# A mixed attention and long-convolution kernel on one core: another order, other slots and other engines for the same 1808 steps

## The chip, the core and the metric

The kernel runs on one core of a Trainium2 chip. The metric is the device time of one execution in microseconds; the median over several executions is compared. The core has a matrix engine (PE, with its weight loads shown apart as PEld), a vector engine (DVE), a scalar engine (ACT), a general engine (POOL), and a sync engine (SP) whose queue issues the transfers here.

## The reference, cut to what matters

Two branches read the same input x (2048 tokens, 512 channels) and a gate per token mixes them.

```
def reference(A_x, A_wq, ..., gate_w):
    def _A_ref(x, wq, wk, wv, wo, beta):       # attention with a memory, 32 heads, 4 segments of 512
        ...
        for s in range(N):
            logits = einsum('bhqd,bhkd->bhqk', qs, ks) * scale + mask
            p = softmax(logits)
            a_dot = einsum('bhqk,bhkd->bhqd', p, vs)
            a_mem = (phi(qs) @ M) / (phi(qs) @ z + 1e-6)
            outs.append(g * a_mem + (1.0 - g) * a_dot)
            M, z = M + phi(ks)^T vs, z + sum(phi(ks))
        return stack(outs) @ wo
    def _B_ref(u, A_re, ..., Dskip):           # a convolution over all 2048 tokens, per channel
        K = einsum('dn,dnl,dn->dl', Cc, exp(dt * A * l), dB).real
        y = irfft(rfft(u padded) * rfft(K padded))[:L]
        return y + u * Dskip
    g = sigmoid((x * gate_w).sum(-1))
    return g * _A_ref(x, ...) + (1 - g) * _B_ref(x, ...)
```

## The kernel before

`build_graph` writes the whole computation down as 1808 steps. A step belongs to an engine and is one instruction on ACT, DVE, POOL or SP, or a short run of matmuls on PE. 611 steps are on PE, 537 on DVE, 142 on ACT, 257 are transfers issued by SP, 6 are on POOL, and 255 are evictions or copies that may run on ACT or on DVE.

A step names the tiles that it reads and writes. A tile lies in a pool with a fixed number of slots (for PSUM, one or two of the eight banks, or four banks for the scores). Nothing decides at run time: the text `ORDER` lists the steps with the slots that each takes for the first time, and for the movable ones the engine, `a` for ACT and `v` for DVE. So `267a` is step 267 on ACT, and `1244/5/0` is step 1244, which takes slot 5 of its first new tile and slot 0 of its second. `replay` walks this list, gives out the slots, and appends each step to its engine's program. `emit` then turns every dependency, on data and on the last users of a slot, into waits on semaphores. Each engine runs its own program in the order of the list; between engines only the semaphores order anything.

The names (tags) of the steps that the text below speaks of:

- `prm`, `dt`, `prep`: the convolution's parameters, their exponentials and sines. `pow0.k` and `pow1.k`: repeated squares (ACT squares, L850; DVE the rest, L851 and L852). `pwc`: their copies to bf16 (L858, L859), with a transfer that swaps halves. `cb`: the products of B and C.
- `xl1.b`: the first step of the transform of x; evictions by `evac` (L229 on ACT, L230 on DVE), then a transfer to a scratch tensor in memory. Two slots take turns. `xTl1` to `xTl3`: x transposed by transfer (L743).
- `tabc0` to `tabc3`, `tab`, `lag`: tables of powers, built by DVE (L1346, L1349, L1355, L1358), and products of them.
- `tok`, `pk`, `pq`, `st`, `gate`: projections, memory state and gate of a segment. `sc`: scores on PE into four banks, exponential on ACT (L1190 and L1237). `mk`: mask on DVE (L1249). `pv`, `nrm`: product with the values and division (L1151 to L1154). `mem`, `oT`: memory read and transposed output.
- `X`, `E`, `K`, `Y`, `V` with 0 to 31: the convolution. X and K are made on PE and evicted, Y is their product on DVE (L1487), V the way back on PE, evicted and moved by a transfer into the tile V2.
- `fin`, `fir`, `fih`, `fis`, `xD`, `spl`, `out` with 0 to 15: the output tiles. `fin` and `fih` are the output projection, `fir` and `fis` the last step of the convolution. Eight of them are split, with a partial sum by DVE (L1521 for xD, L1543 for spl, L1557 for out); the other eight are scaled on their way out by ACT (L232) or DVE (L233).

PE's steps share line L706, the helper that issues a matmul.

## Time and profile before

| | us |
|---|---|
| median of 3 runs | 287.87 |
| lowest and highest | 287.21, 294.32 |
| span of the profiled execution | 287.5 |
| DVE busy in it | 265.0 |
| ACT busy in it | 254.6 |
| PE busy in it | 253.1 |

The profiled execution's span, from its first to its last instruction, is 287.5 us, 0.4 us under the median of the runs. Busy times are sums over one engine's instructions, without overlap. An idle time in the tables stands with what ended it: `7.3 <-PE psum L706 6.0` means 7.3 us of idle time ahead of these instructions, 6.0 of them ended by a matmul.

### The profile page before, as it was taken

The page shows a single profiled execution, that of the slowest core. Times are in us where ns is not written, and L with a number is a line of the kernel's source. Part 1 is how long each engine was busy: PE and PEld are TensorE (multiplying, and loading weights), DVE is VectorE, ACT ScalarE, POOL GpSimd, SP SyncE. Part 2 cuts the span into 40 slices and gives each one's busy share as a digit, 9 for nine tenths or more (in the row PEclk, how much of TensorE's full clock was granted, in tenths as well). Part 3 has the DMA queues.
Part 4 walks back from the last instruction along what each step waited for, and adds up shares of the span by engine and source line. Part 5 has one row for each costly group of instructions (what it writes and reads, how often), then busy time and mean ns, then how long its engine had stood idle before and what let it go on. Part 6 is the DMA issues. An engine that isn't in the chain of part 4 may idle for free.

```text
span 287.5 us, 9336 instructions
## 1 busy us (share of the span) xinstructions
PE 253.1 (88%) x3896; PEld 158.7 (55%) x3947; DVE 265.0 (92%) x617; ACT 254.6 (89%) x320; POOL 5.0 (2%) x10
## 2 busy tenths in 40 slices
PE   5767888787898989979999989999999999999992
PEld 2424454564556546756766657665555454555661
DVE  3998999999999999979999999999999999997782
ACT  5998999999999999989989999999999999983212
POOL 5000000000000000000000000000000000000000
PEclk9999899999999999979999999999999999999999
DMA  6996762421125256914643388585776795894224
GB/s 164 270 223 143 184 203 84 130 87 42 41 47 134 63 141 205 226 32 97 188 132 102 90 252 244 166 232 161 234 215 168 207 229 160 243 186 102 72 109 182
DMA packets 60187, 44.49 MB, mean 155 GB/s; under 512 B 36209, under 2 KB 53490, under 8 KB 60146
## 3 DMA queue, kind: packets, MB, share of 16 engines
q1 hardware_dynamic: 60146, 43.90, 57.0%
q8 instruction: 31, 0.51, 0.8%
q14 instruction: 10, 0.08, 0.1%
HBM read 22.09 MB, written 7.86 MB: 104 GB/s over the span
## 4 chain that ended last, share of the span: by engine, by line
ACT 35%; PE 28%; DVE 26%; issue 5%; DMA 3%; SPq 0%; DVEq 0%; ACTq 0%
PE psum L706 28%; ACT sb L1237 10%; ACT sb L229 10%; ACT sb L1190 8%; DVE sb L1346 7%; DVE sb L1355 3%; ACT sb L850 3%; DVE sb L230 2%; DMA sb<-sb 2%; DVE sb L1349 2%; DVE sb L1487 2%; DVE sb L1358 2%; DVE sb L1249 1%; DVE sb L1154 1%; ACT sb L1021 1%
## 5 line engine op out<-in xcount | busy, mean ns | idle before, releaser
L706 PE MATMUL psum<-sb 128*128 128x17 bf16 (+17 forms) x3808 | 247.4, 229 | 23.5 <-ACT sb L1190 7.4
L706 PEld LDWEIGHTS psum<-sb 128*128 128x128 bf16 (+6 forms) x3859 | 153.5, 102 | 115.5 <-issue 20.7
L229 ACT ACTIVATE sb<-psum 128x512 bf16<-128x512 f32 (+4 forms) x155 | 87.7, 624 | 7.6 <-PE psum L706 6.4
L1237 ACT ACTIVATE sb<-psum 128x2048 bf16<-128x2048 f32 x40 | 76.0, 1899 | 2.1 <-PE psum L706 1.7
L1190 ACT ACTIVATE sb<-psum 128x2048 bf16<-128x2048 f32 (+1 forms) x40 | 70.1, 1751 | 2.8 <-PE psum L706 2.7
L1346 DVE TENSOR_TENSOR sb<-sb 128x4096 bf16<-128x4096 bf16 (+3 forms) x24 | 37.7, 1569 | 0.0
L230 DVE CAST sb<-psum 128x512 bf16<-128x512 f32 (+1 forms) x49 | 29.9, 626 | 1.1 <-PE psum L706 0.9
L1355 DVE TENSOR_TENSOR sb<-sb 128x512 bf16<-128x512 bf16 (+1 forms) x48 | 25.0, 537 | 0.1
L1249 DVE TENSOR_TENSOR sb<-sb 128x1024 bf16<-128x1024 bf16 (+1 forms) x40 | 22.6, 577 | 0.2
L1487 DVE TENSOR_TENSOR sb<-sb 128x1024 bf16<-128x1024 bf16 x32 | 21.6, 685 | 0.9 <-ACT sb L229 0.5
L1349 DVE TENSOR_TENSOR sb<-sb 128x2048 bf16<-128x2048 bf16 (+3 forms) x24 | 20.7, 861 | 0.0
L232 ACT ACTIVATE sb<-psum,sb 128x512 bf16<-128x512 f32 x6 | 4.0, 687 | 12.3 <-PE psum L706 12.3
L1154 DVE TENSOR_TENSOR sb<-psum,sb 128x256 bf16<-128x256 f32 x32 | 13.3, 417 | 0.3
L1358 DVE TENSOR_TENSOR sb<-sb 128x512 bf16<-128x512 bf16 (+1 forms) x24 | 12.9, 536 | 0.0
L850 ACT ACTIVATE sb<-sb 128x512 f32<-128x512 f32 x18 | 11.8, 660 | 0.0
L1151 DVE RECIPROCAL sb<-psum 128x16 f32<-128x16 f32 x32 | 7.9, 252 | 1.8 <-PE psum L706 1.7
L1291 DVE TENSOR_TENSOR sb<-psum,sb 128x512 bf16<-128x512 f32 x12 | 8.2, 687 | 0.2
L858 ACT ACTIVATE sb<-sb 128x512 bf16<-128x512 f32 x12 | 8.0, 683 | 0.0
L1072 ACT ACTIVATE sb<-sb 128x512 bf16<-128x512 bf16 x12 | 8.0, 663 | 0.0
L1021 ACT ACTIVATE sb<-psum 128x512 bf16<-128x512 bf16 x12 | 7.8, 646 | 0.0
L852 DVE SCALAR_TENSOR_TENSOR sb<-sb 128x256 f32<-128x256 f32 x18 | 7.5, 424 | 0.0
L851 DVE TENSOR_TENSOR sb<-sb 128x256 f32<-128x256 f32 x18 | 7.5, 423 | 0.0
(78 smaller groups left out, 122.3 us busy)
## 6 DMA issues: line engine op xcount, KB each, us to landing
sb<-sb SPq DMA_DIRECT2D x64, 128.0 KB, 3.2
sb<-c_DN SPq DMA_DIRECT2D x32, 224.0 KB, 3.0
scr_Z<-sb SPq DMA_DIRECT2D x16, 256.0 KB, 3.2
sb<-scr_Z SPq DMA_DIRECT2D x16, 256.0 KB, 3.6
sb<-in_A_x_dram SPq DMA_DIRECT2D x5, 512.0 KB, 4.6
sb<-c_DN SPq DMA_DIRECT2D x16, 160.0 KB, 3.3
out_dram<-sb SPq DMA_DIRECT2D x8, 256.0 KB, 2.1
scr_O<-sb SPq DMA_DIRECT2D x12, 128.0 KB, 2.7
```

The costliest lines, as they stand in the source:

```text
L229: fa = lambda e: e.activation(dst(), src(), ACT.Copy)
L230: fd = lambda e: e.tensor_copy(dst(), src())
L706: mm = lambda e, o_, l, r_, st, sp, **kw: e.matmul(o_, lhsT=l, rhs=r_, start=st, stop=sp, skip_group_check=True, **kw)
L850: op("ACT", ("As", 512), lambda e, sq=sq, Z=Z: e.activation(ap(sq, n=512), ap(Z, n=512), ACT.Square), r=[Z], w=[sq], key=PW[h] + PWS * k)
L1190: o = op("ACT", ("Ax", 4 * n), lambda e: e.activation(ap(pT, dims=[[512, 4], [1, n]]), ap(P, dims=[[512, 4], [1, n]]), ACT.Exp, scale=0.25 ...
L1237: o = op("ACT", ("Ax", 2048), lambda e, P=P, pT=pT: e.activation(ap(pT, n=2048), ap(P, n=2048), ACT.Exp, scale=0.25), r=[P], w=[pT])
L1249: op("DVE", ("V2", 128 * nb), lambda e, pT=pT, dims=dims: e.tensor_tensor(ap(pT, dims=dims + [[1, 128]]), ap(pT, dims=dims + [[1, 128]]), ...
L1346: op("DVE", ("V2n1" if n == 1 else "V2", 512 * n), lambda e: e.tensor_tensor(ap(tile, 2 * dst, [[2 * (sp - dst), 2], [2 * ne, 128], [1, 2 ...
L1349: op("DVE", ("V2n1" if n == 1 else "V2", 256 * n), lambda e: e.tensor_tensor(D_(), D_(), ap(tile, 2 * sp + ne * 128, [[-ne * 128, 2], [2 * ...
L1355: op("DVE", ("V2x" if sstep > 2 else "V2", 256 * n), lambda e, half=half: e.tensor_tensor(run(t2, n, 0, 1) if half else run(tile, ne, dst, ...
L1358: op("DVE", ("V2", 256 * n), lambda e: e.tensor_tensor(D_(), D_(), ap(t2, n * 128, [[-n * 128, 2], [2 * n, 64], [1, 2 * n]]), ALU.add), r= ...
L1487: op("DVE", ("V2", 1024), lambda e, Y=Y, XAB=XAB, K3=K3, Ke=Ke, xo=xo, u=u: e.tensor_tensor(ap(Y, dims=[[512, 2], [1, 512]]), ap(XAB, xo, ...
```

## The change

The text `ORDER` is replaced by another one; nothing else changes. The 1808 steps, their instructions, the tiles and the pools stay as they are. The list's order is another (1747 of the 1808 positions hold another step), the slots are given out in another way, and of the 255 movable steps 41 change their engine: 23 go from ACT to DVE and 18 from DVE to ACT. They are mostly X, K, V and E evictions of the convolution, and three of the out tiles.

The first lines of both, which hold the head:

```
-9/0 0/0 15/0 16/0 10/1 66/0 29/0 32/0/0 38/1/0 39 33v 41/0 48/1 30/2 31a 40/2 13/2 12/3 47/3 11/4 17/3 43/4 50/5 42/6
-49/7 54/0 44 3/0 51 45 46 56/8 18 19 52 53 215/0 67/4 69/5 55/9 59/0 57/10 58 34/0/1 61/11 70v/0 60/12 64/0 68v 62/13
...
+9/0 15/0 16/0 38/1/0 10/1 39 0/0 32/3/0 33a 48/0 30/2 41/1 31a 40/2 47/3 66/0 11/2 12/3 43/4 50/5 17/0 49/6 44 42/7 51
+45 13/4 22/0 27/0 14/5 46 69/2 7/0 54/0 67/5 4/0 26/0 23/0 52 70v/0 56/8 34/6/1 55/9 1236/1 57/10 53 59/0 58 36/4/2
...
```

And the last lines, with the tail (1736 is spl4, 1714, 1707, 1739, 1790 and 1795 are out1, out0, out4, out12 and out13, 1794 is the last matmul):

```
-1736 1705/5 1706 1707 1744/7 1745/2 1786/1 1762 1731 1715 1763 1805 1806a 1807 1787 1788 1789/1 1746 1738 1739 1791/6
-1792 1790a 1793 1794 1747 1795a 1796
...
+1744/7 1723 1745 1712/2 1746 1706/2 1791/0 1713 1792 1786/6 1736 1731 1774 1793 1714 1787 1788 1789/1 1794 1707 1739
+1763 1715 1747 1790a 1795v 1796
```

The transfers of powers 0 and 1 of the first half are steps 76 and 88; the transposes of x are 399, 626 and 841.

## The prediction

> **What bounds the kernel now.** I read the page's busy times and slices first, then the chain, then the busy time by stretches, then the waits, and last the head and the tail instruction by instruction.

> ```profile
> span 287.5 us, 9336 instructions
> PE 253.1 (88%) x3896; PEld 158.7 (55%) x3947; DVE 265.0 (92%) x617; ACT 254.6 (89%) x320; POOL 5.0 (2%) x10
> ...
> PE   5767888787898989979999989999999999999992
> ...
> DVE  3998999999999999979999999999999999997782
> ACT  5998999999999999989989999999999999983212
> ...
> ACT 35%; PE 28%; DVE 26%; issue 5%; DMA 3%; SPq 0%; DVEq 0%; ACTq 0%
> ```

> Three engines share the bound. DVE alone needs 265.0 of 287.5 us, and neither PE nor ACT is more than 12 us behind it. The slices show where each has room: PE in the first quarter, ACT and DVE in the last tenth. The chain divides itself over all three, so no single wait sets the time; the balance of the list does.

> ```profile
> 20.00:250.00 230.00, 207.80 (x3548) 132.75 (x3593) 223.07 (x531) 223.66 (x274) 1.32 (x2) 0.99 0.57 152
> 250.00:283.00 33.00, 31.91 (x257) 19.29 (x261) 26.57 (x45) 14.47 (x18) 0.00 (x0) 1.00 0.52 143
> 0.00:20.00 20.00, 13.35 (x92) 6.64 (x93) 15.41 (x44) 16.44 (x31) 3.69 (x8) 1.00 0.84 217
> ```

> The columns are length, busy time of PE, weight loads, DVE, ACT and POOL, granted clock, DMA share and GB/s. From 20 to 250 us DVE is idle for 6.9 us (230.0 - 223.1) and ACT for 6.3. From 250 on PE is idle for about 1 us and sets the end.

> ```profile
> 266.98 8.73 PE psum L706 x51
> 275.71 0.06 issue
> 275.77 6.53 PE psum L706 x35
> 282.30 0.02 issue
> 282.32 0.69 ACT sb L232
> ```

> This is the end of the chain: PE without a gap, one eviction of the last output tile, and then 4.5 us (287.5 - 283.0) for the last output transfer.

> **The change, part by part.** No instruction is added or removed. 1747 of the 1808 positions of the list hold another step. Of the 255 evictions and copies that may run on either engine, 23 go from ACT to DVE and 18 from DVE to ACT.

> ```profile
> L229 ACT ACTIVATE sb<-psum 128x512 bf16<-128x512 f32 x135 | 78.0, 628 | 7.3 <-PE psum L706 6.0 <-DMA scr_Z<-sb 1.1
> L230 DVE CAST sb<-psum 128x512 bf16<-128x512 f32 x38 | 25.5, 686 | 1.1 <-PE psum L706 0.9
> L230 DVE CAST sb<-psum 128x256 bf16<-128x256 f32 x11 | 4.5, 418 | 0.0
> ```

> These means overlap the next instruction, so I count what each one adds to its engine's busy time, as the median over the trace: 0.49 us for a 512-wide eviction on ACT, 0.60 on DVE, 0.33 for a 256-wide one on DVE. By that count the 41 swaps take 2.5 us off ACT and put 2.5 us on DVE. If DVE bounded everything the kernel would be 2.5 us longer; if ACT did, 2.5 us shorter. Neither holds over the whole span, so I follow the lists.

> *Sums along the two lists.* Each step gets the time that its own instructions add in this trace. (The sums are PE 255.4, with the pauses inside a step, DVE 265.0, ACT 250.7 without its three table loads of 1.3 us.) I add up each engine's work in the order of the list, old and new. "One engine up to step k of the list, another after it" is then a length that the order wants, if the list's order binds across engines. It binds loosely, since an engine may run ahead of it, so I use differences only and calibrate on the old list.

> - One engine, then another. Old: the largest is DVE up to position 725 and PE after it, 277.8 us (110.1 + 163.3, and 4.4 for DVE's late start). New: DVE up to position 1614 (Y28, 237.9 us of DVE work) and PE after it (35.7 us), 278.0. Looking only at the last quarter: old 243.5 + 28.6 = 272.1, new 273.6, so +1.5.
> - Three stretches. Old: ACT up to 644, DVE to 725, then PE: 282.9. New: ACT up to 231, DVE to 1614, then PE: 282.8.
> - Four stretches that end with an eviction. Old 283.8 (ACT, DVE, PE, ACT), against the 283.0 measured. New 284.9 (ACT, DVE, PE, DVE). The +1.1 comes from the tail: after the matmuls of fin12, DVE still has spl4, out1, out0, out4 and out13 to do (4 x 0.66 + 0.60 = 3.2 us) and PE 5 matmuls of 0.22. In the old list ACT does out13 and DVE is done earlier.
> - Four stretches that end with PE give 287.1 for the old and 285.4 for the new, -1.7.

> So the sums say between -1.7 and +2.5, the last being DVE's added work alone. I take **+1.1**, the sum nearest to the measured end.

> *The head.* The new list issues the DMAs in another order and evicts in another order.

> ```profile
> 13.51 3.61 SPq L743 DMA_TRANSPOSE sb<-in_A_x_dram  x1
> 17.17 0.56 SPq L225 DMA_DIRECT2D sb<-c_mk  x1
> 17.78 1.97 SPq L743 DMA_TRANSPOSE sb<-in_A_x_dram  x1
> 19.79 0.64 SPq L225 DMA_DIRECT2D sb<-sb  x1
> ...
> 25.39 1.58 ACT L229 ACTIVATE sb<-psum 128x512 bf16<-128x512 f32 x3 [1.14 <-DMA scr_Z<-sb]
> ...
> 25.92 0.30 DVE L230 COPY sb<-sb 128x256 bf16<-128x256 bf16 x1 [1.43 <-DMA sb<-sb]
> ```

> ACT waits here 1.14 us for the slot of an xl1 tile, whose transfer was late in SP's queue, and DVE 1.43 us for the swapped half of a power tile. In the new list the next user of either xl1 slot stands later on ACT: about 4 us after the transfer for xl1.3, 0.7 us for xl1.0. Power 3's first reader (tab0.1) stands after 19.6 us of DVE work, its transfer after 15.2, so about 1.4 us are left after 3 us of landing. In the three-stretch sum ACT carries the head of the new list, so I take its whole wait: **-1.1**. The bounds are -1.4 (DVE's wait too) and 0 (the wait comes back behind another slot). The cover is thin in one place: the copies of powers 0 and 1 are now issued behind two of the x transposes, where the old list had power 0's ahead of both. 18 issues of 0.54 us, then 3.6 + 0.6 + 2.0 + 0.6 + 0.6, put power 1's issue at about 18 us and its landing at 21; DVE has 16 us of work ahead of its reader and starts at 5.2. That hides it by a hair. If it doesn't, the reader (tabc0) stands in DVE's queue with pow0.5, the gates and cb1 behind it, and ACT waits for those.

> *The slots.* Counted on the lists, in mean engine work between a PSUM bank's last reader and the step that fills it again, 61 of 598 refills were tight (below nothing) and 169 are now. In the other direction the median distance from a PE step to its ACT reader grows from 0.1 to 1.1 us, and reuse of SBUF slots with less than nothing between falls from 36 to 11. An order in which readers come later and refills come sooner moves the waits from ACT and DVE to PE. What ACT's waits cost is in the rows; what PE's would cost, the next rows bound.

> ```profile
> PE psum L706 <- ACT sb L1190: 7.4, 17, 0.9
> ...
> PE psum L706 <- ACT sb L229: 4.3, 9, 1.4
> ...
> PE psum L706 <- ACT sb L1237: 0.8, 2, 0.4
> PE psum L706 <- DVE sb L1023: 0.4, 1, 0.4
> ```

> A PE wait is 0.4 us (7.4 / 17). Of the tight refills 11 stood after position 1614, where PE sets the pace, and 20 do now: at most 9 x 0.4 = 3.6 us there. Against it stand ACT's and DVE's 13.2 us of idle time in 20 to 250 us, of which the longer distances to the readers can give back up to DVE's 6.9. I take **0** for both together, since both come from one shift of the list; the bounds are -6.9 and +3.6.

> **Sum**: 287.5 + 1.1 - 1.1 + 0 = 287.5 us as a span. The measured median is 287.87, 0.4 us above the profiled execution's own span, so the forecast as a time is **287.9: no change**. A measurement of this kernel tells about 2% from no change, which is 5.8 us: below 282.1 is faster, above 293.6 slower.

> **The rivals.**

> *A, faster: the waits go.* If the longer distance from PE to its readers takes all of DVE's 6.9 us, 287.5 + 1.1 - 6.9 + 0.4 = **282.1**, just at the bound. For it: ACT's and DVE's idle time is mostly put down to PE in the grouped rows (7.3 <-PE 6.0), and DMA waits shrink as well. Against it: DVE has 2.5 us more to do, and the three-stretch sum that ends on DVE (DVE to 1614, PE to 1790, DVE: 280.2, with 4.5 for the last output 284.7, and no idle time in it at all) stands above it. It takes an engine that runs ahead of the list.

> *B, slower: PE waits for banks and its clock drops.* The place is PE's queue from 40 us on, the price per event is in these rows.

> ```profile
> 126.00:130.00 4.00, 3.96 (x53) 3.15 (x47) 3.62 (x12) 2.84 (x4) 0.00 (x0) 0.57 0.20 43
> ...
> 122.00:126.00 4.00, 2.33 (x61) 1.63 (x61) 2.87 (x13) 3.60 (x6) 0.00 (x0) 1.00 0.06 18
> ```

> After 4 us in which PE was busy for 2.33 only, it gets a granted clock of 0.57 for the next 4: about 1.7 us lost on PE, and ACT and DVE idle for 1.5 us between them. The old list has this once after the head. With 169 tight refills instead of 61, four more such stretches cost 4 x 1.7 = 6.8: 287.9 + 6.8 = **294.7**. It decides from the fourth on. For it: the count; three engines near 97% pass every PE pause on. Against it: PE is above 90% busy from 140 us on, far from the 58% that set it off. [...]

> *C, a late transfer at the head.* If power 1's copy lands behind the transposes, DVE stands for up to the 2.0 us of the second transpose, all of it ahead of DVE's long stretch: 287.9 + 2.0 = **289.9**, within 2%. That the change does nothing because engines ignore the list is no rival: each engine's program is this list.

> **How the numbers follow.** Forecast 0.42, A 0.24, B 0.29, C 0.05. A stands on the bound, a little over half of it beyond: faster 0.13. B is slower: 0.29. The rest is 0.58 within 2%. The range reaches to A's end and over B's: 282.5 to 295.

> **What would show it.** Right: DVE busy 267 to 268 us, ACT about 252; the 1.14 and 1.43 us waits at 24 to 26 us gone; at the end DVE, not PE or ACT, runs last, with spl4, out1, out0, out4, out13 back to back. A: idle time of DVE from 20 to 250 us below 2 us. B: several dips of the clock after 40 us, PE's waits for evictions well above the 12 us of the rows here. Wrong: a single long DVE or ACT wait on a transfer that these lists don't show, or a tail in which PE stands.

## The result, and the profile after

The new list is slower: 309.15 us median (306.72 to 310.95, 4 runs) against 288.12 (4 runs, on the same chip), ratio 1.074, 95% interval 1.068 to 1.081. The forecast was 287.9, with 282.5 to 295 as its range. (A ratio below leaves out runs that took over 1.5% longer than the fastest of the same kernel, so it can be smaller than the quotient of its medians.)

The page of the new kernel, first the span and the busy times, then the granted clock by slices, last the chain:

```profile
span 308.6 us, 9336 instructions
PE 265.6 (86%) x3896; PEld 164.2 (53%) x3947; DVE 266.6 (86%) x622; ACT 255.7 (83%) x315; POOL 5.0 (2%) x10
...
PEclk9989778975759999997999999999999999999999
...
PE 33%; ACT 22%; DVE 17%; DMA 15%; issue 6%; SPq 4%; DVEq 0%; ACTq 0%
```

DVE and ACT have as much to do as before, within 2 us. PE's busy time rose by 12.5 us for the same matmuls, so matmuls have become longer (234 ns in the mean of L706's, 229 before), and the clock row says where: slices 5 to 12, 31 to 93 us. Busy time by stretches (columns as in the prediction: length, PE, weight loads, DVE, ACT, POOL, clock, DMA share, GB/s), first of the new kernel, then of the old one:

```profile
60.00:80.00 20.00, 17.30 (x304) 11.06 (x299) 15.01 (x46) 13.25 (x17) 0.00 (x0) 0.66 0.23 63
80.00:100.00 20.00, 16.24 (x265) 10.29 (x260) 17.44 (x32) 17.63 (x24) 0.00 (x0) 0.74 0.15 37
```

```profile
60.00:80.00 20.00, 16.07 (x315) 10.49 (x315) 19.59 (x41) 19.70 (x28) 0.00 (x0) 1.00 0.17 48
80.00:100.00 20.00, 17.82 (x411) 12.12 (x413) 19.78 (x58) 20.00 (x25) 0.66 (x1) 1.00 0.36 86
```

In these 40 us the old list keeps DVE and ACT at work for 39.4 and 39.7 us, the new one for 32.4 and 30.9, with PE as busy (33.5 and 33.9 us) and at half clock for 24 of the 40 us. Lining up both traces where the three engines have added the same work gives the **lag** of a kernel, told here at the old kernel's time. For the new one it is 3.7 us at 20 us, 3.9 at 36, 6.3 at 57, 16.2 at 92, 16.5 still at 189, 20.1 at 216 and 21 at the end. So there are a head, a middle and a tail, and the middle (57 to 92 us) is half of it.

The waits, of the new kernel (engine and line that wait, what for, total us, times, longest):

```profile
ACT sb L229 <- PE psum L706: 16.0, 19, 2.9
...
PE psum L706 <- ACT sb L1190: 9.3, 19, 1.4
ACT sb L1190 <- PE psum L706: 7.4, 12, 2.3
...
DVE sb L1151 <- PE psum L706: 5.8, 4, 3.6
```

and ACT's of the old one:

```profile
ACT sb L229 <- PE psum L706: 6.4, 7, 1.8
ACT sb L1190 <- PE psum L706: 2.7, 7, 0.5
...
ACT sb L1237 <- PE psum L706: 1.7, 4, 0.7
```

PE hardly waits longer for its evictions (9.3 us for L1190, 7.4 before). It is its readers that wait for a slower PE.

### The profile page after: what moved, and what is told of

Its sections match the earlier page's. It is cut to its first block, busy times and chain, and to the rows that moved or that the text cites. A ratio compares the mean times of both kernels' runs of the same rounds, so it can differ in the third digit from the quotient of the medians.

```text
span 308.6 us, 9336 instructions
## 1 busy us (share of the span) xinstructions
PE 265.6 (86%) x3896; PEld 164.2 (53%) x3947; DVE 266.6 (86%) x622; ACT 255.7 (83%) x315; POOL 5.0 (2%) x10
## 4 chain that ended last, share of the span: by engine, by line
PE 33%; ACT 22%; DVE 17%; DMA 15%; issue 6%; SPq 4%; DVEq 0%; ACTq 0%
PE psum L706 33%; ACT sb L1190 10%; ACT sb L229 8%; DMA sb<-sb 7%; DVE sb L230 3%; SPq L225 3%; DMA sb<-c_DN 3%; DVE sb L1346 2%; ACT sb L1237 2%; DMA scr_O<-sb 2%; DVE sb L1487 2%; DVE sb L1249 2%; DMA sb<-in_A_wk_dram 2%; DVE sb L1355 1%; DMA sb<-scr_Z 1%
## 5 line engine op out<-in xcount | busy, mean ns | idle before, releaser
L706 PE MATMUL psum<-sb 128*128 128x17 bf16 (+19 forms) x3808 | 260.1, 234 | 35.2 <-ACT sb L1190 9.3
L706 PEld LDWEIGHTS psum<-sb 128*128 128x128 bf16 (+6 forms) x3859 | 158.6, 104 | 133.5 <-issue 32.2
L229 ACT ACTIVATE sb<-psum 128x512 bf16<-128x512 f32 (+5 forms) x150 | 84.6, 607 | 19.1 <-PE psum L706 16.0
L1237 ACT ACTIVATE sb<-psum 128x2048 bf16<-128x2048 f32 x40 | 75.4, 1885 | 4.8 <-PE psum L706 4.3
L1190 ACT ACTIVATE sb<-psum 128x2048 bf16<-128x2048 f32 (+1 forms) x40 | 69.1, 1728 | 7.7 <-PE psum L706 7.4
L230 DVE CAST sb<-psum 128x512 bf16<-128x512 f32 (+2 forms) x55 | 34.4, 635 | 3.1 <-PE psum L706 2.7
L232 ACT ACTIVATE sb<-psum,sb 128x512 bf16<-128x512 f32 x7 | 4.6, 685 | 12.1 <-PE psum L706 12.1
L1154 DVE TENSOR_TENSOR sb<-psum,sb 128x256 bf16<-128x256 f32 x32 | 13.2, 414 | 0.3
L1543 DVE SCALAR_TENSOR_TENSOR sb<-psum,sb 128x512 f32<-128x512 f32 x8 | 5.9, 746 | 3.9 <-PE psum L706 3.9
```

What stands on the lines that cost most here:

```text
L229: fa = lambda e: e.activation(dst(), src(), ACT.Copy)
L230: fd = lambda e: e.tensor_copy(dst(), src())
L706: mm = lambda e, o_, l, r_, st, sp, **kw: e.matmul(o_, lhsT=l, rhs=r_, start=st, stop=sp, skip_group_check=True, **kw)
L1154: op("DVE", ("V1", 256), lambda e: e.tensor_tensor(ap(o1, gi * 16, [[128, 4], [32, 4], [1, 16]]), ap(T, dims=[[68, 4], [17, 4], [1, 16]]), ...
L1190: o = op("ACT", ("Ax", 4 * n), lambda e: e.activation(ap(pT, dims=[[512, 4], [1, n]]), ap(P, dims=[[512, 4], [1, n]]), ACT.Exp, scale=0.25 ...
L1237: o = op("ACT", ("Ax", 2048), lambda e, P=P, pT=pT: e.activation(ap(pT, n=2048), ap(P, n=2048), ACT.Exp, scale=0.25), r=[P], w=[pT])
```

## The experiments

The theory: the half clock in the middle makes most of the loss, and the clock falls because too little of the array is in use in the windows before. Its rivals: the loss sits in the head and the rest inherits it; it is waits that the order makes, and the clock only shows them; the 41 engine swaps cost it. (Each expectation numbers its own theories.) "Half clock" is the sum of the stretches with a granted clock of 0.5 in the profiled execution, the last of 2 to 5 us at its very end included; for the old kernel 9.6 us, for the new one 43.1. A window is 3.41 us: in the traces of both kernels every stretch that is on record at one clock, 1.00 or 0.50, lasts a whole number of these (1 to 48), but for the piece at the end.

| kernel | time, us (before beside it) | ratio, 95% | half clock |
|---|---|---|---|
| oldhead640 | 297.71 (289.97) | 1.024, 1.010 to 1.038 | 18.6 |
| newhead640 | 308.79 (289.97) | 1.062, 1.048 to 1.077 | 45.9 |
| oldhead250 | 304.50 (289.97) | 1.048, 1.033 to 1.062 | 39.6 |
| new_fill | 312.93 (289.97) | 1.076, 1.059 to 1.094 | 34.4 |
| new_fill3 | 311.02 (290.54) | 1.071, 1.059 to 1.083 | 24.8 |
| new_oldmid | 304.96 (290.54) | 1.050, 1.041 to 1.059 | 33.3 |
| oh640_oldletters | 310.21 (290.54) | 1.064, 1.054 to 1.073 | 28.2 |
| oh640_wolate | 299.16 (290.54) | 1.025, 1.015 to 1.035 | 18.6 |
| new_headq | 305.33 (289.83) | 1.040, 1.030 to 1.051 | 32.6 |
| old_fill3 | 298.83 (289.83) | 1.030, 1.023 to 1.036 | 6.9 |
| new_oldletters | 320.29 (289.83) | 1.108, 1.101 to 1.115 | 28.2 |
| old_newletters | 312.28 (289.83) | 1.075, 1.067 to 1.082 | 25.7 |
| new_fill3r16 | 336.66 (289.58) | 1.155, 1.143 to 1.166 | 91.9 |
| headq_oldmid | 306.75 (289.58) | 1.066, 1.058 to 1.073 | 37.3 |

**Which part of the list.** Three lists are put together from the two. Each step keeps the engine letter of the list that its place comes from, and in newhead640 three steps (558 to 560) stand 16 or fewer places later. No run changes the slots alone; they go with the order.

```
oldhead640:  old[:640] + the rest in the new order
newhead640:  new[:640] + the rest in the old order
oldhead250:  old[:250] + the rest in the new order
```

> The first 640 steps in the old list's order (to about 102 us), all others in the new list's. The trace of after is 16 us behind before at equal work by then and loses another 5 us later. Theory 1 (the loss sits in the first third, where PE's clock is halved) says 288 + 5 = 293 us, with at most two half-clock stretches before 100 us. Theory 2 (the new list is tight at bank refills everywhere) says the loss goes with the share of the list: about 302 us.

> The first 640 steps in the new list's order, all others in the old list's. Theory 1: 288 + 16 = 304 us, with the half-clock stretches of after before 100 us. Theory 2: about 295 us.

> The first 250 steps in the old list's order (to about 39 us), all others in the new list's. If the late transfers of the head (3.7 us behind at 23 us) also set off the slow stretch from 57 to 100 us, that stretch goes as well: about 294 us. If the slow stretch comes from the order of the steps in it, only the head's 3 to 4 us are won: about 305 us.

The first 640 steps carry most of it: with them old, 297.7, between the two expectations; with them new, 308.8, above both and nearly as slow as the whole new list. The clock rows of the two, in that order:

```profile
PEclk9988999999999996999999999999799999999998
```

```profile
PEclk9989778975759999799999999999999999999998
```

oldhead640 is 0.4 us behind at 92 us, gets 3 around the seam (106 to 120 us) and 3.5 at 204 to 210 us, the tail's part. oldhead250, 304.5, has no lag at 36 us and 10.4 at 85: the middle loses by its own order, without the slow head, so it doesn't inherit the loss.

**The clock.** Added matmuls that nobody needs, written into banks ahead of the real ones, raise the use of the array and cost PE's time. Steps of segment 0 only:

```
new_fill:   16 score steps:  + 2 x mm(P, ident[:, :128], kT[:, :512])         6.9 us of PE
new_fill3:  all 20 score steps, + the same 512 columns in pv and lag steps   12.1 us of PE, 56 matmuls
old_fill3:  the same 56 matmuls in the old list
new_fill3r16: new_fill3 with the added matmuls on 16 rows (one of the three places):
-   mm(e, ap(P, n=512), ap(ident, n=128), ap(kT, n=512), True, True)
+   mm(e, ap(P, n=512), ap(ident, n=128, np_=16), ap(kT, n=512, np_=16), True, True)
```

> After, with two more 512-column matmuls at the head of 16 of the 20 score steps of the first segment (the real ones overwrite their result): 32 x 0.216 = 6.9 us more work for PE between 28 and 102 us. Theory 1 in its sharper form, that the clock halves after a stretch of 3.4 us in which the array streams too little, says that the half-clock stretches between 28 and 95 us (34 us of them) mostly go and the time falls to 299 to 304 us although PE has more to do. The rival, that the clock follows PE's pauses or the waits only, says the time rises to 309 to 316 us.

> After, with 512-column matmuls whose results are overwritten, spread more evenly over the stretch from 28 to 102 us: two at the head of each of the 20 score steps of the first segment, one ahead of each first product with the values there, two ahead of each bank of lag0: 56 x 0.216 = 12.1 us more work for PE. The traces so far say that a window of 3.41 us in which the array streams less than about 0.30 of its area-time is followed by a window at half clock (24 of 25 windows), above 0.40 almost never (1 of 419). Theory 1 says that with no window under 0.33 left before 102 us, at most two half-clock windows remain there (12 in after) and the time falls below that of after, to 298 to 306 us, although PE does 12 us more. If the half clock is a by-product and the waits are the cause, the time rises by up to 12 us, to 312 to 321 us.

> The old list with the same 56 extra matmuls of 512 columns in segment 0 (12.1 us of PE's time) that brought the new list to 311.0. This is the control that says what the added work costs where the clock is full anyway. Theory 1 (in the new list the matmuls took away half clock that was worth about 10 us and cost about as much themselves): the old list pays for them in full, since nothing comes back: 296 to 301, with no less half clock than the 9.6 us that it has now. Theory 2 (the extra matmuls fill idle time of PE and cost nearly nothing, and half clock costs nearly nothing either): 288 to 292.

> The new list with the same 56 added matmuls of 512 columns in segment 0 as the run with no half clock between 46 and 257 us (311.0 us), but reading 16 rows of the array and not 128: the same 12.1 us of PE's time at full clock, an eighth of the array's work. Theory 1 (the clock follows how much of the array is used in a window of 3.41 us): the half clock comes back between 46 and 105 us, 20 us of it or more, and since half clock doubles the added matmuls too, the time is 317 to 326. Theory 2 (the clock follows PE's busy time or its pauses, which the added matmuls fill in either form): no more than 7 us of half clock between 46 and 105 us, and 309 to 313.

new_fill, 312.9, fell in the rival's range: the added matmuls lifted too few windows (34.4 us of half clock are left). new_fill3 took the half clock away altogether from 46 to 257 us, though four such windows stayed ahead of that where two were expected, and still ran 311.0, between the two expectations. Alone that decides nothing; the control helps: in the old list the same matmuls cost 9.0 us (298.83 - 289.83), as its theory 1 had it (its half clock fell to 6.9 us, which theory 1 did not expect). Spans of the profiled executions: new 308.6, new_fill3 311.2, so the added work of 9.8 (297.3 - 287.5) came with 18.3 us less half clock and a gain of 7.2: **0.39 us for each us of half clock**. These are single executions on different chips; with the medians, each against the old kernel on its own chip, the gain is 9.5 us (9.0 + 21.0 - 20.5) and the price 0.5. So this pair gives an estimate. The last kernel has the same instructions at the same places as new_fill3, with an eighth of the rows. Clock rows of new_fill3, then of new_fill3r16:

```profile
span 311.2 us, 9442 instructions
...
PEclk9779779999999999999999999999999995999998
```

```profile
span 337.3 us, 9495 instructions
...
PEclk9989676955575557799999999899999999999999
```

67.1 us more half clock and 26.1 us more time: 0.39 again. (What the added matmuls take longer at half clock, 0.427 us for 0.216 by the new kernel's trace, is in that.) The two quickest executions of new_fill3r16 (spans of 329.6 and 332.3 us, mean clocks 0.891 and 0.882) against the two of new_fill3 (307.2 and 311.2, 0.976 and 0.963) give 0.39 as well. The time, 336.7 and at the least 331.6, lies above the 317 to 326 of its theory 1. Between 46 and 105 us, 45 of the 59 us are at half clock, where its theory 1 asked for 20 or more and its theory 2 for 7 at most. And PE was as busy as can be; these are the windows of new_fill3r16 ahead of two falls and behind them:

```profile
42.58:45.99 3.41, 3.41 (x74) 2.51 (x67) 2.86 (x8) 3.41 (x6) 0.00 (x0) 1.00 0.40 99
45.99:49.41 3.42, 3.42 (x43) 2.61 (x36) 2.75 (x4) 2.25 (x3) 0.00 (x0) 0.50 0.02 5
93.79:97.20 3.41, 3.41 (x51) 1.86 (x43) 1.06 (x3) 3.31 (x6) 0.00 (x0) 1.00 0.02 5
97.20:100.61 3.41, 3.15 (x51) 1.85 (x49) 3.38 (x7) 2.27 (x5) 0.00 (x0) 0.50 0.09 19
```

PE is busy for 3.41 of 3.41 us, and the next window runs at half clock. In new_fill3 it pauses for a quarter of a window and keeps its clock (the array use defined below is 0.30 in this window, against 0.29 and 0.26 ahead of the two falls, so the comparison speaks against busy time and shows no threshold):

```profile
83.61:87.02 3.41, 2.54 (x46) 1.57 (x45) 3.41 (x5) 3.33 (x7) 0.00 (x0) 1.00 0.19 43
87.02:90.43 3.41, 3.25 (x57) 2.01 (x55) 3.17 (x9) 3.04 (x5) 0.00 (x0) 1.00 0.52 138
```

So busy time is not the measure here. The one that fits these traces is the sum over a window's matmuls of columns x rows / 128 x weight columns / 128 (128 x 128 are the largest weights in them), over 8192. A window holds about that many columns at full clock: a matmul of 512 columns follows the one before it by 0.216 us there (by 0.427 at half clock), which makes 3.41 / 0.216 x 512 = 8083. Here is one window of the new kernel whose next one ran at half clock, and its matmuls by form (rows*columns of the weights, then rows x columns streamed):

```profile
59.26:62.68 3.42, 2.65 (x67) 1.81 (x69) 3.07 (x8) 3.42 (x5) 0.00 (x0) 1.00 0.02 5
62.68:66.09 3.41, 3.41 (x50) 2.79 (x52) 2.34 (x10) 3.13 (x4) 0.00 (x0) 0.50 0.52 130
```

```profile
L706 PE MATMUL psum<-sb 32*128 32x448 bf16 x8 | 0.9, 445 | 0.6 <-ACT sb L1190 0.6
L706 PE MATMUL psum<-sb 128*64 128x17 bf16 x14 | 0.8, 178 | 0.2 <-issue 0.2
L706 PE MATMUL psum<-sb 128*128 128x17 bf16 x12 | 0.5, 171 | 0.0
L706 PE MATMUL psum<-sb 128*64 128x34 bf16 x8 | 0.4, 187 | 0.0
L706 PE MATMUL psum<-sb 128*128 128x128 bf16 x4 | 0.4, 220 | 0.0
L706 PE MATMUL psum<-sb 128*128 128x512 bf16 x1 | 0.4, 390 | 0.0
L706 PE MATMUL psum<-sb 128*32 128x1 bf16 x16 | 0.3, 167 | 0.0
L706 PE MATMUL psum<-sb 32*128 32x64 bf16 x4 | 0.2, 188 | 0.0
```

896 (8 x 448 / 4) + 119 + 204 + 136 + 512 + 512 + 4 + 64 = 2447, over 8192: 0.30 (0.29 without the six that only end there), where PE is busy for 2.65 of 3.42 us, 0.78. The scores read 32 rows, the products with the values stream 17 columns: busy PE, idle array. The old kernel has the same thin matmuls: its five windows below 0.40 between 57 and 92 us have a use of 0.33 to 0.39, with PE busy for 0.81 to 0.94. The new kernel's three windows ahead of a fall there have 0.27 to 0.29, with PE busy for 0.75 to 0.80. All windows of the 16 traces, counted that way by the matmuls that start in them:

```
array use of a window    at full clock: next one at half    at half clock: next one at half
below 0.30                       46 of 49                          36 of 37
0.30 to 0.35                     20 of 35                          13 of 16
0.35 to 0.40                      8 of 48                           9 of 28
0.40 to 0.45                      2 of 78                           0 of 24
0.45 and above                    0 of 991                          0 of 29
```

Of the full-clock windows with PE busy for 0.75 or more but array use below 0.30, 10 of 10 are followed by half clock; of those with PE busy below 0.65 but array use of 0.40 or more, 2 of 25. Busy time sorts them nearly as well as long as nothing is added: of 820 full-clock windows with PE busy for 0.90 or more, two are followed by half clock, both in new_fill3r16; but of 88 half-clock windows with PE busy for 0.95 or more, 34 are. The counts are a correlation; the pair of new_fill3 and new_fill3r16, which differ in rows alone, is the test. It tests the rows. That the weight columns belong in the product is not tested: without them the falls from full clock are sorted nearly as well (28 of 29 below 0.30, 2 of 1070 at 0.45 and above).

**The middle and the head.**

```
new_oldmid:   new[:250] + what is left of old[:640], in its order + the rest new
new_headq:    new list; the 27 SP transfers of its first 130 steps in the old list's order, but for step 76
headq_oldmid: new_headq[:250] + what is left of old[:640] + the rest new
```

> The first 250 steps as in after, then what is left of the old list's first 640 in the old order, then the rest as in after. It keeps the new head and the new end. If the order of the steps between 250 and 640 makes the slow stretch, 298 to 301 us and few half-clock windows from 57 to 100 us; if the new head makes it, as in after, 306 to 310 us.

> The new list with one edit: the 27 transfers that SP issues within its first 130 steps come in the order that they have in the old list (the weights for k and v ahead of those for q, the copies of powers 0 and 1 ahead of nothing but one transpose of x); the order on PE, ACT and DVE is the new one, step for step. The new kernel ran 3.7 us behind the old one at 23 us, with PE waiting 3.1 us for the weights of k. Theory 1 (the order of SP's queue makes the loss at the head): the lag at 23 us falls below 1 us and the wait for the weights of k goes; with the stretches of half clock from 57 to 102 us left as they are, the time is 305 to 306; if they go as well, 296 to 298. Theory 2 (the head's loss is in the order of the engines, and each load only shows it): the lag at 23 us stays at 3 us or more, with a wait for another load (the weights of q) in its place, and the time is 308 to 310.

> The new list with two of its parts undone: SP's first transfers in the old order (as in the run that showed 1.2 us of lag at 36 us) and, after the first 250 steps, the rest of the old list's first 640 steps in their old order; the last 1168 steps are the new ones. Theory 1 (the losses of the head, of the middle and of the tail are separate and add up): 4 us or less behind the old kernel at 100 us, and with the tail's 4 to 7 us 295 to 299, as with all of the first 640 steps old (297.7). Theory 2 (any seam or mixture costs by itself, and the middle loses as much in another order): 300 or more, with a lag of 8 us at 100 us as with the new head and the old middle (305.0).

In new_headq the copy of power 0 (step 76) still stands behind two transposes of x, with that of power 1, and not ahead of both as in the old list. In the new list SP issues the weights of q first, and the transposes of x hold its queue. SP's own rows of the new kernel and, below, of new_headq:

```profile
4.81 1.07 SPq L225 DMA_DIRECT2D sb<-in_A_wq_dram  x1
...
9.10 0.52 SPq L225 DMA_DIRECT2D sb<-in_A_wk_dram  x1
...
11.50 6.73 SPq L743 DMA_TRANSPOSE sb<-in_A_x_dram  x1
```

```profile
7.33 0.51 SPq L225 DMA_DIRECT2D sb<-in_A_wk_dram  x1
...
9.51 0.49 SPq L225 DMA_DIRECT2D sb<-in_A_wq_dram  x1
10.05 5.61 SPq L743 DMA_TRANSPOSE sb<-in_A_x_dram  x1
```

PE's wait for the weights of k goes from 3.1 to 1.8 us. new_headq's lag is still 3.2 us at 20 us, as its theory 2 had it, but only 1.2 at 36 us (new: 3.9). So in this execution the kernel has 2.7 us back by then, later than theory 1 said; the two half-clock windows that the new kernel has before 36 us are missing in it as well, and the run does not part the queue from the clock. It then loses 10.8 us up to 92 us all the same. new_oldmid, 304.96, fell between its two expectations. It loses 2.2 us from 50 to 92 us where the new list loses 9.9, and has 6.8 us of half clock from 57 to 100 us where the new list has 23.9: the middle's own order is worth 7 to 8 us. But the two don't add up. headq_oldmid has a lag of 4.7 us at 36 us already and of 9.4 at 92, with 27 us of half clock in six stretches from 22.9 to 128.6 us: 306.75, no better than either. Its theory 2 held. Its first 250 steps are those of new_headq, whose profiled execution has no half clock before 39 us; here there are two windows of it. So the same steps had half clock in one execution and none in another, and new_headq's own four times reach from 299.75 to 309.56, with mean clocks of 0.961 and 0.938. The parts can be ranked by such runs, not added to a tenth.

**The engines.**

```
old_newletters:   the old list; the 41 swapped steps on the new list's engines
new_oldletters:   the new list; the same steps on the old list's engines
oh640_oldletters: oldhead640 with the old list's engines
```

> The old list with the engines of the new one for the 41 movable steps that changed theirs; order and slots are the old ones. Theory 1 (engines and order were chosen together): slower than the old kernel by 5 us or more, 293 to 305, with engines waiting for each other in 120 to 250 us where most of the swapped evictions stand. Theory 2 (the swaps cost what they add to DVE): 288 to 290.5, DVE's busy time about 267.5 us.

> The new list with the engines of the old one for the 41 movable steps that changed theirs (23 back from DVE to ACT, 18 from ACT to DVE). Theory 1 (engines and order were chosen together, so that the old engines don't fit the new order): slower than the new kernel by 5 us or more, 314 to 325. Theory 2 (the swaps are a cost of their own, 2.5 us more on DVE, as the prediction counted): faster than the new kernel by up to 2.5 us, 306 to 308.

> The list with the old first 640 steps and the new rest (297.7 us), with the old choice of ACT or DVE for every movable step. The prediction's term says that the swaps put 2.5 us more on DVE: 295.2 us if DVE bounds the last two thirds, 297.7 if the choice does not matter there, later than 298 if the new order was made for the new choice.

Theory 1 of the first two held (old_newletters lost more than its 293 to 305): engines and order belong together. 41 of 1808 steps on the other engine, with not one step moved, make the **old** list 22 us slower, as much as the whole change. Its stretches, and those of before:

```profile
150.00:200.00 50.00, 43.26 (x632) 26.59 (x631) 41.53 (x109) 41.76 (x44) 0.66 (x1) 0.93 0.51 138
200.00:250.00 50.00, 44.39 (x517) 23.51 (x515) 43.43 (x101) 42.05 (x44) 0.00 (x0) 0.97 0.62 172
```

```profile
150.00:200.00 50.00, 47.81 (x743) 31.05 (x751) 48.47 (x128) 49.85 (x57) 0.00 (x0) 1.00 0.64 179
200.00:250.00 50.00, 48.65 (x621) 26.86 (x628) 48.77 (x115) 49.25 (x52) 0.00 (x0) 1.00 0.73 201
```

All three engines are idle for 5.6 to 8.5 us in each 50, which I read so, without having followed single steps: an eviction that changed its engine stands there behind steps that are not due yet, PE doesn't get its bank, and the other engine doesn't get its matmul. ACT's waits in old_newletters:

```profile
ACT sb L229 <- PE psum L706: 17.1, 17, 4.1
ACT sb L1237 <- PE psum L706: 11.2, 15, 2.4
```

They were 6.4 and 1.7 us. The loss comes nearly all after 165 us (2.3 us behind at 162, 23.4 at 278), and at 0.39 us each the 16 us more of half clock would be 6 of the 22, an estimate; here the waits do most. The new list needs its own letters too: with the old ones it takes 320.3 (314.1 to 322.0). And oldhead640 with the old ones goes from 297.7 to 310.2: its first 640 steps keep pace, then it loses 5 us at 155 to 162 us and more from there, so the new order from position 640 on is made for the new letters.

**A load that could have been in the way.** Where the tail loses, the new kernel has its DMA engines at their densest (first row; the share is the last but one), more so than the old one (second), and the 512 KB of wo are in it:

```profile
200.00:220.00 20.00, 16.97 (x240) 10.90 (x245) 17.70 (x44) 17.45 (x21) 0.00 (x0) 1.00 1.06 222
```

```profile
200.00:220.00 20.00, 19.80 (x234) 11.24 (x236) 19.44 (x49) 19.82 (x24) 0.00 (x0) 1.00 0.68 196
```

```
oh640_wolate: oldhead640; ld_wo moved from position 1206 to 1623 of the list
```

> The same list (297.7 us), with the one 512 KB load of the output weights moved from position 1206 to 1623, near its old place: out of the stretch around 200 us, where the transfers are densest. If this load delays the convolution's transfers behind it, the 3.5 us lost around 205 to 212 us go: about 294.5 us. If not, 297.7.

299.16 (294.89 to 300.60) against 297.71 for oldhead640: no gain is seen, and the load is not shown to be the cause of the tail's loss.

## Why the prediction was wrong, by its own steps

- **"I take 0 for both together"** (slots and banks) is the step that failed first. The count of tight refills, 61 to 169, pointed the right way, but it was priced as waits of 0.4 us each. PE's waits for L1190 rose by 1.9 us only. What the runs show in its place is the clock: with PE paused a little longer among the same thin matmuls the array's use falls below 0.30 (0.27 to 0.29 in the three windows ahead of a fall), one half-clock window costs 3.41 x 0.39 = 1.3 us, and the next one can be low as well: two stretches of 10.2 us at half clock. That it was the tight refills that made these pauses is not shown.
- **Rival B** had the drop of the clock and about its price (1.7 us a stretch; 1.3 us a window by the estimate above) and the wrong number: four windows, where 33.5 us more of half clock are ten. Its trigger was wrong too. "PE above 90% busy from 140 us on, far from the 58% that set it off" looked at busy time; all but one of the half-clock windows, and the piece at the end, lay before 94 us, some of them behind a window with PE busy for 0.78. The row it went by, 122 to 126 us, could not tell busy time from use: the window in it ahead of the fall has PE busy for 0.51 and a use of 0.30. Being busy is not the measure in these traces, by the 3.41 of 3.41 us ahead of a half-clock window in new_fill3r16, and by the same rows no pause of PE in the window ahead is needed for a fall.
- **The swaps, "2.5 us off ACT and 2.5 us on DVE"**, were priced by busy time: wrong in kind. The busy time did move (DVE 265.0 to 266.6, less than the 267 to 268 forecast), but the same swaps alone cost 22 us in the order that they don't belong to.
- **The sums along the lists, +1.1**, hold no clock and no wait inside a stretch. They gave 282.8 to 284.9 for the two lists, and both did take longer than that; as a difference they carried nothing.
- **The head, -1.1**, had the wrong sign: +3.7 us by 20 us. ACT's wait of 1.14 us for the xl1 slot went, as said, and so did DVE's of 1.43 us for the copy of power 3. But the waits of the head are others now. PE waits 3.07 us for wk, ACT 2.79 us for the two products with it, and DVE 3.05 us for a square that stands behind their evictions on ACT. The step looked at waits that were there, not at what the new order of SP's queue makes late: wk at 9.10 us, where the old kernel has the second row.

```profile
18.73 0.43 DVE L851 TENSOR_TENSOR sb<-sb 128x256 f32<-128x256 f32 x1 [3.05 <-ACT sb L850]
```

```profile
7.22 0.51 SPq L225 DMA_DIRECT2D sb<-in_A_wk_dram  x1
```

- **Rival C**, put at 0.05, came true beside B: DVE's copy of power 1 (step 1037 of tabc0) waits 1.64 us for the swapped half, of the 2.0 us that C allowed. Power 1's transfer was to be issued at about 18 us and was issued at 22.3, the second of these two, since the first transpose holds the queue for 6.73 us, not 3.61. In new_headq, which issues the two 3 us earlier, DVE has no such wait.

```profile
21.53 2.43 SPq L225 DMA_DIRECT2D sb<-sb  x2
...
26.48 0.30 DVE L230 COPY sb<-sb 128x256 bf16<-128x256 bf16 x1 [1.64 <-DMA sb<-sb]
```

- **The tail** went as told: DVE ends it with spl4, out1, out0, out4 and out13, in these rows; it cost nothing, since PE's last matmul ends at 303.3 us as well.

```profile
300.54 0.74 DVE L1543 SCALAR_TENSOR_TENSOR sb<-psum,sb 128x512 f32<-128x512 f32 x1
301.20 2.06 DVE L1557 SCALAR_TENSOR_TENSOR sb<-psum,sb 128x512 bf16<-128x512 f32 x3
303.36 0.75 DVE L233 TENSOR_SCALAR sb<-psum,sb 128x512 bf16<-128x512 f32 x1
```

- **The signs it named for B** were half right: the clock dipped many times, before and after 40 us, but PE's waits for evictions hardly grew. Its readers' waits did (ACT L229 on PE, 6.4 to 16.0 us), against the forecast that longer distances to the readers would shorten them.

The account, as far as it goes: of 21 us, 33.5 us of half clock at 0.39 make 13, an estimate from the two pairs of fill runs, where most of the half clock that differs lay in 46 to 131 us (at the 0.5 of the first pair's medians it would be 17). The other 8, or 4, would be waits: some at the head, where the late transfers and two half-clock windows are not parted, some in the middle, and some at 189 to 216 us of the old kernel's time, where the new one falls back 3.6 us at full clock. What makes that last part is not settled. Neither is why these steps in this order pause first, ahead of any half clock. The runs show that the order between positions 250 and 640 makes most of the half clock from 57 to 92 us and of the lag there, and that no combination tried beats the old list.

## What to carry to other kernels

Before an order is changed, work out PE's array use window by window (columns x rows x weight columns over a window of 3.41 us), not its busy share: here a stretch of scores with 32 rows and of products with 17 columns was 0.78 busy and 0.30 used, and of the 49 full-clock windows with a use below 0.30 in the 16 traces 46 were followed by half clock, so that a pause of another engine may be paid a second time by the clock, 1.3 us a window by the estimate above. A list, its slots and its engine letters are one solution: price an engine swap by what stands ahead of it in the other engine's queue, and expect a mixture of two orders to be worse than its parts say. Sums of busy time lay below the measured time of both lists and said nothing of the difference between them.
